# The quotients' steps of an attention kernel, one period each

## The chip, the cores and the metric

The kernel runs on one core of a Trainium2 chip. The metric is the device time of one execution in microseconds. Three runs of the kernel before took 1059.01, 1059.93 and 1061.18 us; the median is 1059.93. All times inside the execution are counted from its first instruction.

## The reference

Linear attention over 8 batches of 8 heads (576 positions, 64 dimensions, 128 features), and behind it a two-layer network on the 4608 rows that the attention gives. In the kernel the division of the attention stands in the middle of a long pipeline.

```python
def _attn_ref(q, k, v, w_phi):
    def phi(x):
        proj = np.einsum('bhsd,df->bhsf', x, w_phi)
        proj = proj - np.max(np.abs(proj), axis=-1, keepdims=True)
        return np.concatenate([np.exp(proj), np.exp(-proj)], axis=-1)
    q_p, k_p = (phi(q), phi(k))
    kv = np.einsum('bhsf,bhsd->bhfd', k_p, v)
    z = np.sum(k_p, axis=2)
    num = np.einsum('bhsf,bhfd->bhsd', q_p, kv)
    den = np.einsum('bhsf,bhf->bhs', q_p, z)[..., None] + 1e-06
    return (num / den)

def _moe_ref(x, w_in, w_out):
    h = x @ w_in
    return (h - np.tanh(h)) @ w_out
```

## The kernel before

Two heads of one batch make a unit; there are 32 units, numbered from 0. The attention stage is a software pipeline over the units. `ramp` starts the first three, `period(i)` for i from 3 to 31 does one step each of several units, `drain` ends the last five and starts the matrix stage. The order of the instructions on each engine is the order in which the program writes them (`manual_schedule`), so each engine and SyncE's DMA queue work strictly in that order.

In `period(i)` unit a = i is projected by TensorE (`project`, L327) and centred by VectorE (`centre`, L345 and L346); unit c = i - 1 gets its exponentials on ScalarE (`k_exp`, `q_exp`), its kv product on TensorE (`kv`, L409) and its key sums: GpSimd adds five blocks with four additions (`kadd`, L419 to L422), and one period later TensorE sums over the partitions (`ksum`, L428). Unit p = i - 2 gets its numerator (`num`, L456). Unit r = i - 3 gets its denominator (`denom`, L470).

From there the quotients run. `denom_copy` (ScalarE, L487) writes the denominators to the tile `dd`, of which there is one. `den_recip_load` (SyncE, L492) moves them to `dn`, spread over 128 partitions. `den_recip` (VectorE, L497) makes the reciprocals `rn`, `den_store` (SyncE, L502) writes them to DRAM as `rr`, `den_spread` (SyncE, L507, two DMAs) reads them back as `rb`, each head's row repeated over 64 partitions; there is one `rb`. `den_mul` (GpSimd, L510) multiplies the numerator `d` by `rb`, and `x_store` (SyncE, L513) writes the product to DRAM. The numerator comes to `d` by `num_copy` (ScalarE, L483); there are three buffers `d`, and a fourth for every fourth unit.

Before the change these steps lie in the periods of a unit u as follows. Load, reciprocal and store of the quotients are in period u + 3: the reciprocal is VectorE's last instruction of the period, and behind it stands the centring of the next one. The spread is in period u + 4, in SyncE's queue behind the load of dn. The product and its store are in period u + 5: the product stands on GpSimd ahead of the additions, the store at the head of SyncE's queue, ahead of the qk load.

SyncE's queue also holds the loads of q and k (`load`, L303, two periods ahead), of v (`load_v`, L307), of the raw weights (`dec_load`, L267 and L272) and, by `aside_at`, the stores of prepared weights (L112). The raw weights are decoded on ScalarE and VectorE (`dec_0` to `dec_3`); GpSimd prepares sums of weights between its other work (L168), and near the end sums of the stored products (`x0_sum`). `dn`, `rn` and the raw weights have two buffers each.

In the matrix stage (`frame`, one after another) the last two units' reciprocal, store, spread, product and store are put in by `hooks`.

Of the kernel before, what the change touches and what calls it, by code (L numbers as in the profile page):

```python
# [33 lines left out]
def tile_linear_attention_moe(  # L34
# [192 lines left out]
    with ExitStack() as c1:  # L227
# [287 lines left out]
        units = []  # L515
# [144 lines left out]
            k_exp(c, 0)  # L660

        def period(i):
            a, c, p, r, q, o = (unit(i - n) for n in range(6))
            w = dec[i - 3]
            dec.append(dec_load(i - 2))
            if i > 3:
                num_copy(r)
            k_exp(c, 1)
            if o:
                den_mul(o)  # L670
                x_store(o)
            if i + 2 < NU:
                load(units[i + 2])
            project(a, "jat")
            centre(a, "jt")
            kadd(c)
            ksum(p, p.pc[:, 0:F])
            ksum_copy(p)
            pu = bank()
            denom(r, pu)  # L680
            denom_copy(r)
            den_recip_load(r)
            if q:
                den_spread(q)
            if i > 3:
                load_v(a)
            aside_at(i, 2)
            aside_at(i, 3)
            kv_turn(p)
            ksum_turn(p, p.pc[:, F : 2 * F])  # L690
            kv_turn_copy(p, nc.scalar.copy)
            ksum_turn_copy(p)
            dec_0(w, a.pt)
            if i < NU - 1:
                aside_at(i, False)
            aside_at(i, True)
            q_turn(c)
            q_turn_rest(c, pu)
            q_exp(c)
            q_exp_rest(c)  # L700
            centre(a, "a")
            k_exp(a, 0)
            kv(c)
            kv_copy(c)
            dec_1(w)
            dec_2(w)
            dec_3(w)
            if r:
                den_recip(r)
                den_store(r)  # L710
            num(p)

        splits, lows, early_u = [], {}, {}

        def drain():
            o, q, r, p, c = units[-5:]

            def op(m):
                lows[m] = x_op(0, m, nc.vector)

            def pt_bank():
                return ps_t.tile([P, 2, 512], F32, tag="pt", name="pt")

            k0 = order[5]
            k_exp(c, 1)
            dec.append(dec_load(NU - 2))
            den_mul(o)
            ksum(p, p.pc[:, 0:F])
            ksum_copy(p)
            pu = bank()  # L730
            denom(r, pu)
            denom_copy(r)
            den_recip_load(r)
            ring_store(k0, 2)
            x0_sum(3)
            kadd(c)
            x_store(o)
            den_spread(q)
            kv_turn(p)
            ksum_turn(p, p.pc[:, F : 2 * F])  # L740
            kv_turn_copy(p)
            ksum_turn_copy(p)
            v = dec[NU - 3]
            dec_0(v, pt_bank())
            num_copy(r)
            x0 = xop[0][0]
            nc.scalar.copy(x0[:, 0], f32(x0[:, 1]))
            dec_1(v)
            dec_2(v)
            dec_3(v)  # L750
            x_low(nc.vector, x0, f32(x0[:, 1]))
            den_recip(r)
            den_store(r)
            q_turn(c)
            q_turn_rest(c, pu)
            q_exp(c, (0,))
            kv(c)
            kv_copy(c)
            q_exp(c, (1,))
            q_exp_rest(c)  # L760
            c0.close()
            xoa = ctx.enter_context(tc.tile_pool(name="xoa", bufs=1, side="right", reuse_waits="tile"))
            for s in XO_NEXT:
                xop_pool[s] = xoa
            ps_ab.append(ctx.enter_context(tc.tile_pool(name="ps_ab", bufs=1, side="right", reuse_waits="tile", space=PSUM)))
            num(p)
            kv_turn(c)
            kv_turn_copy(c)
            num_copy(p)
            pu = bank()  # L770
            denom(p, pu)
            denom_copy(p)
            den_recip_load(p)
            x1 = xop[0][1]
            nc.vector.tensor_copy(x1[:, 0], f32(x1[:, 1]))
            x_low(nc.vector, x1, f32(x1[:, 1]))
            w = dec[NU - 2]
            dec_0(w, pt_bank())
            dec_1(w)
            op(2)  # L780
            num(c)
            dec_2(w)
            dec_3(w)
            ksum(c, pu[:, 0:F])
            ksum_copy(c)
            den_mul(q)
            x_store(q)
            den_spread(r)
            op(3)
            lows[2]()  # L790
            bank_ab(0, ps_ab[0], "AB")
            product(A[0], 0, 0, 0, True)
            ksum_turn(c)
            u = early_u[0, "u1"] = wpool.tile([P, DM], F32, tag="w", name="u1_0")[:, 0:HT]
            nc.scalar.copy(u, A[0][:, 0:HT])
            ksum_turn_copy(c)
            product(Bk[0], 0, 1, 1, True)
            op(4)
            den_mul(r)
            x_store(r)  # L800
            num_copy(c)
            denom(c, bank())
            denom_copy(c)
            splits.extend(wo_split(f, nc.vector) for f in range(4))
# [10 lines left out]
    with ExitStack() as c2:  # L815
# [371 lines left out]
        def hooks(g, k):  # L1187
            q = NFP * g + k
            h = collections.defaultdict(list)
            nxt = g + 1  # L1190

            def op(at, g, m, low_at):
                keep = []
                h[at].append(lambda: keep.append(x_op(g, m, nc.vector)))
                h[low_at].append(lambda: keep[0]())

            if q + 2 < NQ:
                for n, at in enumerate(("a2", "a5", "end")):
                    h[at].append(lambda n=n: ring_load(q + 2, n))
            if g and k == 0:  # L1200
                op("a4", g, 6, "a6")
            if g and k == 1:
                for t, at in enumerate(("a2", "a2", "a3", "a5", "a5", "a6")):
                    h[at].append(lambda t=t: evict(g - 1, t, nc.vector if t == 1 else nc.scalar))
            if nxt < NG:
                if k == (2 if g else 4):
                    h["end" if g else "a2"].append(lambda: x_loads(nxt))
                if 4 <= k < 7:
                    for n, at in (((0, "a3"), (1, "end")), ((2, "a3"),), ((3, "a3"),))[k - 4]:
                        h[at if g else "end"].append(lambda n=n: x_sum(nxt, n))  # L1210
                    op("a4" if g else "end", nxt, k - 4, "a6" if g else "end")
                if k == 7:
                    op("a2", nxt, 3, "a3")
                    op("a4", nxt, 4, "a6")
                    op("end", nxt, 5, "end")
            if g == 0:
                for p in PREP.values():
                    for kk, at, names in (
(2, "end", "s1 s3 s2 s4"),
                        (3, "a3", "h2 l2 h4"),  # L1220
                        (3, "end", "l4 h6"),
                        (4, "a3", "l6"),
                        (4, "end", "h0 l0"),
                    ):
                        if k == kk:
                            h[at].extend(p[nm] for nm in names.split())
                for kk, at, n in ((3, "a6", 1), (4, "a6", 2), (5, "a1", 0)):
                    if k == kk:
                        h[at].append(lambda n=n: ring_store(NFP - 1, n))
                for kk, at, f in ((2, "end", LATE.d0), (3, "a7", LATE.d1), (5, "a7", LATE.d2), (6, "a7", LATE.d3)):  # L1230
                    if k == kk:
                        h[at].append(f)
                split = {}
                for n, at in enumerate(("a6", "a7")):
                    f = 2 * k + n

                    def hi(f=f):
                        split[f] = wo_split(f, nc.vector)
                        split[f][0]()

                    h["a0"].append(hi)
                    h[at].append(lambda f=f: split[f][1]())
            for n, kk in ((2, 2), (1, 4)):
                if g == 1 and k == kk:
                    h["start"].append(lambda n=n: (den_recip(units[-n]), den_store(units[-n]), den_spread(units[-n])))
                if g == 1 and k == kk + 1:
                    h["end"].append(lambda n=n: (den_mul(units[-n]), x_store(units[-n])))
            return h
# [102 lines left out]
```

## Time and profile before

| | |
|---|---|
| median of the three runs shown | 1059.93 us |
| profiled execution, its own time | 1059.23 us |
| its span, first to last instruction | 1057.4 us |
| around the span | 1.8 us |
| TensorE busy | 1042.4 us, 99% |
| VectorE, ScalarE, GpSimd busy | 870.2, 792.1, 272.8 us |
| attention stage, periods 4 to 31 | begins at 33.03 us; period 31 begins at 284.19 us |
| granted TensorE clock | 0.999 |

The busy time of TensorE is close to the whole span, but its matmuls are pipelined, and a wait shows less as idle time than as a later start of the next period. GpSimd works in the attention stage nearly alone: of the 40 slices of the span the last 27 show 0 tenths for it. In rows of the profile PE is TensorE, PEld its weight loads, DVE VectorE, ACT ScalarE, POOL GpSimd and SP SyncE; a q behind the name is the engine's sequencer or queue.

### The profile page before, as it was taken

How to read it: one execution, taken by the hardware profiler on the slowest of the kernel's cores; microseconds unless marked ns; L12 is line 12 of the kernel's file. 1: busy time of each engine (PE TensorE's matmuls, PEld its weight loads, DVE VectorE, ACT ScalarE, POOL GpSimd, SP SyncE). 2: the span in 40 equal slices, each digit the busy share in tenths (PEclk: the TensorE clock that was granted, in tenths of full speed). 3: DMA queues.
4: the chain of work that ended last, by engine and by line, in shares of the span. 5: the costliest groups of instructions: out<-in, count | busy, mean ns of one | idle time of the engine just before them, and what ended most of it. 6: DMA issues, size and time to landing. Idle time of an engine off the chain costs nothing.

```text
span 1057.4 us, 19349 instructions
## 1 busy us (share of the span) xinstructions
PE 1042.4 (99%) x7484; PEld 874.0 (83%) x7484; DVE 870.2 (82%) x1086; ACT 792.1 (75%) x1281; POOL 272.8 (26%) x233
## 2 busy tenths in 40 slices
PE   8999999999989999999999999999999999999998
PEld 6666666666668998999999999999999999999997
DVE  7899888889979899878887788867887778877776
ACT  5888888988878778766777666776677667776665
POOL 4799899989960000000000000000000000000000
PEclk9999999999999999999999999999999999999999
DMA  5789999999847653464335433345334543353311
GB/s 166 205 233 282 264 271 288 267 272 270 253 142 263 201 187 103 159 216 144 121 120 190 167 131 122 120 169 179 128 106 156 199 137 113 120 180 109 123 47 60
DMA packets 75738, 184.59 MB, mean 175 GB/s; under 512 B 15744, under 2 KB 30464, under 8 KB 75648
## 3 DMA queue, kind: packets, MB, share of 16 engines
q1 hardware_dynamic: 75360, 183.17, 53.9%
q8 instruction: 59, 0.97, 0.4%
q14 instruction: 31, 0.25, 0.1%
q10 hardware_dynamic: 288, 0.20, 0.1%
HBM read 149.49 MB, written 33.70 MB: 173 GB/s over the span
## 4 chain that ended last, share of the span: by engine, by line
PE 82%; DMA 7%; DVE 5%; ACT 2%; POOL 2%; issue 1%; SPq 1%; ACTq 0%; DVEq 0%; POOLq 0%
PE A L142 18%; PE B L142 14%; PE po L987 12%; PE po L988 12%; PE po L993 12%; DMA dn<-dd 4%; PE po L456 3%; PE pc L409 3%; DVE t L346 2%; PE pj L327 2%; PE pa L327 2%; PE pu L470 2%; DVE m L345 1%; DMA rb<-rr 1%; DMA rr<-rn 1%
## 5 line engine op out<-in xcount | busy, mean ns | idle before, releaser
L142 PE MATMUL A<-xo,wr 128*128 128x384 f32 x1152 | 231.5, 337 | 0.0
L142 PEld LDWEIGHTS A<-xo,wr 128*128 128x128 f32 x1152 | 204.9, 188 | 11.4 <-ACT d L483 0.5
L911 ACT COPY u<-A 128x384 f32<-128x384 f32 x143 | 68.5, 479 | 142.6 <-PE A L142 142.2
L142 PE MATMUL B<-xo,wr 128*128 128x384 f32 x864 | 173.7, 337 | 0.0
L142 PEld LDWEIGHTS B<-xo,wr 128*128 128x128 f32 x864 | 152.5, 188 | 4.2 <-DVE hx L918 0.4
L987 PE MATMUL po<-who,ghx 128*128 128x512 f32 x288 | 112.3, 390 | 0.7 <-ACT hy L925 0.7
L987 PE MATMUL po<-who,ghy 128*128 128x512 f32 x288 | 112.3, 390 | 0.3 <-ACT ghy L962 0.3
L988 PE MATMUL po<-wlo,ghx 128*128 128x512 f32 x288 | 112.0, 389 | 0.0
L988 PE MATMUL po<-wlo,ghy 128*128 128x512 f32 x288 | 112.0, 389 | 0.0
L510 POOL TENSOR_TENSOR d<-d,rb 128x576 f32<-128x576 f32 x32 | 46.3, 1448 | 165.4 <-DMA rb<-rr 160.8
L950 DVE SCALAR_TENSOR_TENSOR s2y<-s2y,thy 128x768 f32<-128x768 f32 x48 | 46.0, 959 | 51.5 <-ACT thy L941 51.5
L398 ACT ACTIVATE kp<-t 64x256 f32<-64x256 f32 (+1 forms) x126 | 85.1, 722 | 2.1 <-DVE t L346 1.0
L993 PE MATMUL po<-who,glx 128*128 128x512 f32 x288 | 80.9, 389 | 0.0
L935 ACT ACTIVATE yx<-hx 128x768 f32<-128x768 f32 (+1 forms) x49 | 41.0, 836 | 52.9 <-DVE hx L918 52.9
L993 PE MATMUL po<-who,gly 128*128 128x512 f32 x282 | 79.3, 389 | 0.3 <-DVE gly L965 0.3
L409 PE MATMUL pc<-kp,v 128*64 128x256 f32 x640 | 76.1, 384 | 0.5 <-DMA v<-in_v 0.4
L456 PE MATMUL po<-qe,kv 128*64 128x288 f32 x512 | 69.0, 412 | 0.4
L993 PEld LDWEIGHTS po<-who,glx 128*128 128x128 f32 x288 | 54.0, 188 | 11.2
L947 DVE SCALAR_TENSOR_TENSOR s2x<-s2x,yx 128x768 f32<-128x768 f32 (+1 forms) x49 | 46.1, 941 | 20.4 <-ACT s2x L936 19.1
L993 PEld LDWEIGHTS po<-who,gly 128*128 128x128 f32 x282 | 52.8, 188 | 11.7 <-DVE gly L965 0.8
L987 PEld LDWEIGHTS po<-who,ghx 128*128 128x128 f32 x288 | 54.1, 188 | 8.8 <-ACT hy L925 1.1
L987 PEld LDWEIGHTS po<-who,ghy 128*128 128x128 f32 x288 | 54.1, 188 | 8.5 <-ACT ghy L962 0.7
(186 smaller groups left out, 2228.8 us busy)
## 6 DMA issues: line engine op xcount, KB each, us to landing
wr<-wd SPq DMA_DIRECT2D x92, 512.0 KB
wr<-wd SPq DMA_DIRECT2D x46, 768.0 KB
qk<-in_qkT SPq DMA_DIRECT2D x31, 576.0 KB
v<-in_v SPq DMA_DIRECT2D x32, 320.0 KB
rb<-rr SPq DMA_DIRECT2D x64, 144.0 KB
xs<-d SPq DMA_DIRECT2D x32, 288.0 KB
out<-o SPq DMA_DIRECT2D x35, 256.0 KB
rawi<-in_moe_w_in SPq DMA_DIRECT2D x16, 512.0 KB
```

The costliest lines, as they stand in the source:

```text
L142: nc.tensor.matmul(bank[:, 0:HT], w[:, a, n, cs], x[:, b, c, :], start=start and i == 0, stop=i == 5, skip_group_check=not start,)
L327: nc.tensor.matmul(bank[:, e, k * F : (k + 1) * F], u.qk[hs, a * P : (a + 1) * P], wph[hs, :], start=True, stop=True)
L398: nc.scalar.activation(u.kp[h, :, j, s, :], u.t[r][h, :, x, :], AF.Exp, scale=1.0 - 2.0 * s)
L409: nc.tensor.matmul(u.pc[e * D : (e + 1) * D, 0 : 2 * F], u.v[:, j, e, :], u.kp[:, e, j, :, :], start=(j == first), stop=(j == last))
L456: nc.tensor.matmul(u.po[e * D : (e + 1) * D, c, 0:CH], u.kv[:, s, e * D : (e + 1) * D], u.qe[:, e, s, c * CH : (c + 1) * CH], start=(s == ...
L510: pin(nc.gpsimd.tensor_tensor(u.d, u.d, u.rb, ALU.mult))
L911: nc.scalar.copy(t, A[q][:, 0:HT])
L947: nc.vector.scalar_tensor_tensor(z.s[:, s], z.s[:, s], GC, z.y[:, s], ALU.add, ALU.mult)
L950: nc.vector.scalar_tensor_tensor(z.s[:, s], z.s[:, s], GK, z.th[:, s], ALU.mult, ALU.mult)
L987: nc.tensor.matmul(po, z.gh[:, ts], wh, start=first, stop=False)
L988: nc.tensor.matmul(po, z.gh[:, ts], wl, start=False, stop=False)
L993: nc.tensor.matmul(po, z.gl[:, ts], wh, start=False, stop=last)
```

## The change

In `period` the steps of the quotients move. The reciprocal and its store now serve unit q = i - 4 and stand ahead of the decoding of the weights; the spread serves unit o = i - 5 and stands near the head of SyncE's queue; the product of unit o stands behind the additions; the store of the product serves unit z = i - 6 and stands ahead of the spread. The load of dn stays with unit r but goes behind the load of v and the weight stores. `drain` and `hooks` are changed to fit: the drain makes the reciprocals of units 28 and 29, and the matrix stage gets the spread, the product and the store of unit 29.

```diff
         def period(i):
-            a, c, p, r, q, o = (unit(i - n) for n in range(6))
+            a, c, p, r, q, o, z = (unit(i - n) for n in range(7))
...
             k_exp(c, 1)
+            if z:
+                x_store(z)
             if o:
-                den_mul(o)
-                x_store(o)
+                den_spread(o)
...
             kadd(c)
+            if o:
+                den_mul(o)
...
             denom_copy(r)
-            den_recip_load(r)
-            if q:
-                den_spread(q)
...
             aside_at(i, 3)
+            den_recip_load(r)
...
             kv_copy(c)
+            if q:
+                den_recip(q)
+                den_store(q)
             dec_1(w)
             dec_2(w)
             dec_3(w)
-            if r:
-                den_recip(r)
-                den_store(r)
             num(p)
...
         def drain():
-            o, q, r, p, c = units[-5:]
+            z, o, q, r, p, c = units[-6:]
...
             dec.append(dec_load(NU - 2))
-            den_mul(o)
+            x_store(z)
+            den_spread(o)
...
             kadd(c)
-            x_store(o)
-            den_spread(q)
+            den_mul(o)
...
-            den_recip(r)
-            den_store(r)
+            den_recip(q)
...
             den_recip_load(p)
+            den_store(q)
+            x_store(o)
+            den_spread(q)
...
             x_store(q)
-            den_spread(r)
...
-            den_mul(r)
-            x_store(r)
+            den_recip(r)
+            den_store(r)
             num_copy(c)
...
-            for n, kk in ((2, 2), (1, 4)):
+            for n, kk in ((3, 0), (2, 2), (1, 4)):
                 if g == 1 and k == kk:
-                    h["start"].append(lambda n=n: (den_recip(units[-n]), den_store(units[-n]), den_spread(units[-n])))
+                    h["start"].append(lambda n=n: (n < 3 and (den_recip(units[-n]), den_store(units[-n])), den_spread(units[-n])))
```

## Rows read from the trace of the kernel before

**Rows 1.** The page: the chain that ended last, shares of the span by line.
```profile
PE A L142 18%; PE B L142 14%; PE po L987 12%; PE po L988 12%; PE po L993 12%; DMA dn<-dd 4%; PE po L456 3%; PE pc L409 3%; DVE t L346 2%; PE pj L327 2%; PE pa L327 2%; PE pu L470 2%; DVE m L345 1%; DMA rb<-rr 1%; DMA rr<-rn 1%
```

**Rows 2.** Waits from 30 to 292 us: us in total, times, longest.
```profile
POOL d L510 <- DMA rb<-rr: 11.7, 16, 1.8
...
DVE rn L497 <- DMA dn<-dd: 9.1, 11, 1.3
```

**Rows 3.** Timeline of TensorE, first projections of five periods: start us, us, instruction.
```profile
33.03 0.38 PE L327 MATMUL pj<-wph,qk 64*128 64x128 f32 x2
...
60.31 0.38 PE L327 MATMUL pj<-wph,qk 64*128 64x128 f32 x2
...
209.42 0.38 PE L327 MATMUL pj<-wph,qk 64*128 64x128 f32 x2
...
219.39 0.38 PE L327 MATMUL pj<-wph,qk 64*128 64x128 f32 x2
...
284.19 0.38 PE L327 MATMUL pj<-wph,qk 64*128 64x128 f32 x2
```

**Rows 4.** Timeline of VectorE and ScalarE; in brackets the idle time before.
```profile
211.44 0.22 DVE L497 RECIPROCAL rn<-dn 128x9 f32<-128x9 f32 x1 [1.34 <-DMA dn<-dd]
...
287.91 0.50 ACT L487 ACTIVATE dd<-pu,bias_t 128x288 f32<-128x288 f32 x1 [0.70 <-PE pu L470]
...
289.91 1.23 DVE L346 TENSOR_TENSOR t<-pa,m 128x1024 f32<-128x1024 f32 x1
```

**Rows 5.** Timeline of SyncE's queue in one period: the issues, not the transfers.
```profile
211.68 0.32 SPq L502 DMA_DIRECT2D rr<-rn  x1
...
214.81 0.39 SPq L303 DMA_DIRECT2D qk<-in_qkT  x1
...
215.97 1.87 SPq L507 DMA_DIRECT2D rb<-rr  x2
217.90 0.58 SPq L307 DMA_DIRECT2D v<-in_v  x1
```

**Rows 6.** Chain from 30 to 292 us, DMA pieces: start, us until its waiter.
```profile
107.95 2.83 DMA rr<-rn
...
126.63 5.09 DMA rr<-rn
...
204.86 6.49 DMA dn<-dd
...
215.29 5.69 DMA dn<-dd
...
272.59 4.95 DMA rb<-rr
```

**Rows 7.** Timeline of ScalarE and GpSimd: exponentials, first addition.
```profile
214.33 1.30 POOL L419 TENSOR_TENSOR ss<-kp 128x512 f32<-128x512 f32 x1
...
284.97 2.00 ACT L398 ACTIVATE kp<-t 128x1024 f32<-128x1024 f32 x2
```

**Rows 8.** Timeline of the drain, several engines.
```profile
294.88 0.43 PE L428 MATMUL pc<-ss,ones 128*32 128x128 f32 x8 [1.52 <-POOL ss L422]
...
296.55 1.41 POOL L510 TENSOR_TENSOR d<-d,rb 128x576 f32<-128x576 f32 x1
...
304.69 1.86 POOL L422 TENSOR_TENSOR ss<-ss,kp 128x512 f32<-128x512 f32 x1
...
306.61 0.43 PE L428 MATMUL pu<-ss,ones 128*32 128x128 f32 x8 [1.09 <-POOL ss L422]
...
307.97 0.33 SPq L513 DMA_DIRECT2D xs<-d  x1
...
309.59 0.65 ACT L483 COPY d<-po 128x576 f32<-128x576 f32 x1
...
310.49 1.32 PE L142 MATMUL A<-xo,wr 128*128 128x384 f32 x6
```

**Rows 9.** Busy time of a period: PE, PEld, DVE, ACT, POOL, clock, DMA share, GB/s.
```profile
115.66:125.83 10.17, 9.29 (x119) 6.13 (x118) 8.33 (x12) 8.32 (x16) 9.33 (x10) 1.00 0.95 255
```

## The prediction

> **What bounds the kernel now.** I read the chain of waits of the whole span first: it is matrix work nearly throughout, with one foreign entry in front, the load dn<-dd with 4% of the span, some 40 us [rows 1]. That is not yet 40 us to win, because the chain follows a load back to its issue, past matrix work that ran meanwhile. So second the list of waits of the attention stage, which tells what the engines really lost: VectorE's reciprocal waited 9.1 us in 11 periods for that load, and GpSimd's product 11.7 us in 16 periods for the spread quotients [rows 2]. Third, TensorE's first projection of each period, as a ruler. From 33.03 to 60.31 three periods took 27.28 us, 9.093 each; the one that begins at 209.42 took 9.97 [rows 3], and in that one the reciprocal stood idle for 1.34 us before it ran at 211.44 [rows 4]. VectorE works in order and centres the next projections behind the reciprocal, so TensorE gets its transposes late. About half a microsecond of each such wait is swallowed (1.34 became 0.88), because VectorE is that far ahead of TensorE in a period without a wait. Over all: 284.19 - 33.03 = 251.16 us for 27 periods, against 27 x 9.093 = 245.51. **5.65 us** is all that TensorE loses in the steady periods.
>
> Why the load is late: it stands in SyncE's queue behind the store of the product and the big qk load. The one for the reciprocal at 211.44 was issued at 204.86 and ended 6.49 us later, the longest such piece of the chain; the next, issued at 215.29, took 5.69 [rows 4, 6]. Behind the last period lies a second limit: in the drain TensorE waits 1.52 us at 294.88 and 1.09 us at 306.61 for GpSimd's additions, which run behind a product of 1.41 us [rows 8].
>
> **The change, part by part.** Nothing is added to the steady periods: one reciprocal, one store, two spreads, one product and one store of the product each, as before. They move. Times below are from a period's first projection.
>
> *Reciprocal.* It runs one period after its load, behind the last centring. That ends at 289.91 + 1.23 - 284.19 = +6.95 [rows 3, 4]. The load of the period before is issued by SyncE behind spread, qk, v and up to two weight stores: the new quotient store leaves at +7.19 (6.95 + 0.22, then 0.02 as between 211.66 and 211.68) and lands R later, so the next period's spread starts at R - 1.90; with 1.87 for the spread, 0.39 for qk, 0.58 for v and 0.58 for each weight store as a bound, the load leaves at R + 2.10 and lands D later [rows 5]. R is 2.83 to 5.09, D 5.69 to 6.49 [rows 6]: at worst +13.7, and the reciprocal wants it at 9.09 + 6.95 = +16.0. The wait goes, with 2.4 us to spare; its 0.22 us now lies ahead of the weight decoding, whose result is needed a period later. What is late next on VectorE is TensorE's projection itself. Gain 5.65 us.
>
> *Spread at the period's head.* Before it, SyncE holds the weight load and the store of an already finished product; behind it queue qk, v, the weight stores and dn. It waits until the quotient store has landed, +0.9 to +3.2. qk left at 214.81, +5.4, before, because SyncE stood before the product's store until GpSimd had multiplied; now at most at R - 1.90 + 1.87 = +5.1. Two periods lie between that load and its use. Cost nothing; the cover is those buffers.
>
> *Product behind the additions.* The additions can start when ScalarE's exponentials are done, 284.97 + 2.00 - 284.19 = +2.8, where they started at 214.33, +4.9 [rows 7]. Four of 1.3 us end near +8.2. The spread lands by about +0.9..3.2 plus 4.95 [rows 6] and its second issue, 1.4: +7.3 to +9.6. GpSimd may idle 1.4 us before the product, a wait that it had before (11.7 us in 16). The product's store is a period later; its buffer is wanted by the number copy at the next period's start, some 7 us after. Nothing either way.
>
> *DMA work.* A period of 10.17 us with the engines 0.95 busy holds 9.66 us of transfers [rows 9], more than 9.09. There the stage cannot come down to the ruler: 0.57 us comes back. Bounds: nothing (buffers even it out) to 1.5 us (its neighbours too).
>
> *Drain.* Of the two products that stood before the additions of the last two units one goes behind them, 1.41 us. In the last but one period the product now precedes the weight and input sums instead, so I count 1.0 us of earlier end for the last additions (bounds 0 and 1.41). A new wait stands against it: the product of the unit numbered 27 now follows those additions (end E = 304.69 + 1.86 = 306.55), its store leaves at E + 1.45 as at 307.97, and the last unit's copy d<-po at 309.59 (E + 3.04) reuses its buffer. TensorE's product at 310.49 waits for that copy's bank [rows 8]. No row shows the landing of such a store; between its issue of 0.3 and the 2.83 of the quickest small store [rows 6] it costs 0 to 1.24 us. I take the middle, 0.6. Drain: -0.4, bounds -1.4 to +1.2. The product and the store of unit 29 move into the matrix stage, where GpSimd is idle; its reciprocal stays in the drain, later, and costs at most its 0.22 us, which I put at nothing.
>
> The addition at 304.69 took 1.86 us, the one at 214.33 1.30 [rows 7, 8]. The Trainium skill ("GPSIMD Engine Reference", 1. Specifications) says that GpSimd shares its SBUF interfaces with VectorE and contends with instructions that have two SBUF inputs; the trace agrees as far as the length of this row goes. By that rule the additions, now beside other VectorE work, could all take 1.86, which would leave 0.6 us less.
>
> **Sum.** -5.65 + 0.57 - 0.4 = -5.5 us. The profiled execution took 1059.23 (span 1057.4 and 1.8 around it), so 1053.7; the median shown is 0.70 higher, which makes 1054.4. I forecast 1054.1.
>
> **Rivals.** *A, the wait moves (chance 0.12).* Part of the wait comes back as a late spread or as full DMA engines. For it: 9.66 us of transfers in the longest period [rows 9]. Against: that is the longest, and the loads have one to two periods of lead. If half of the 5.65 stays: about 1057.
>
> *B, slower: SyncE's queue as a loop (0.08).* Spread, qk, v, weight stores and dn all stand behind one landing. dd has one buffer, so ScalarE's copy at 287.91, +3.72 [rows 4], may not start before dn has been read: R + 2.10 + D must stay under 9.09 + 3.72 = 12.81, R + D under 10.7. Behind that copy are the kv and key-sum copies that TensorE waits for. With both longest rows, 5.09 + 6.49 = 11.58, each of 25 periods is 0.87 longer, 22 us: 1076. The change loses from R + D = 10.71 + 5.5/25 = 10.93 on. Against: 2.83 + 5.69 = 8.5 are the lower rows. The Trainium skill ("DMA: Bandwidth & Descriptors", Latency and other measured facts) puts the fixed cost of a DMA at about 2 us, higher under load; with 2 us each the rival could not occur, but the rows show two to three times that.
>
> *C, no change (0.10).* The reciprocal's waits go, but the same half microsecond is lost elsewhere, because VectorE or the DMA engines were late anyway; 1059 to 1060. Against: the periods without a wait keep 9.09 with the same work. Here belongs also that the load, issued later, still comes too late; the 2.4 us speak against it.
>
> Forecast 0.70. Its own range is 1052.5 to 1056.5, from the bounds of the drain and of the DMA term. About 0.2% or 2.1 us is what a measurement of this kernel can tell from no change. Faster by more: the forecast and most of A, 0.81. Within: C and the rest of A, 0.11. Slower: B, 0.08. The range 1051.9 to 1057.6 takes in A.
>
> **What would show it.** Right: no idle time before the reciprocal, a ruler of 9.09 from the fifth period on, 245.5 to 246.5 us for the 27 periods; additions starting near +2.9; the product's idle time small; in the drain a short wait of the last copy d<-po for a store. Wrong: idle time of ScalarE before dd for a load (B), of TensorE for v or qk (A), or a ruler that stays at 9.3 with nothing waiting for dn (C).

## The result and the profile after: slower by 1.3%

The changed kernel takes 1074.65 us (median of 4 runs, 1071.52 to 1076.05) beside 1060.56 us of the kernel before on the same chip (4 runs): ratio 1.0128, 95% interval 1.0100 to 1.0156. Forecast were 1054.1 us and "faster". The case that came is rival B, which had a chance of 0.08, with a second loss in the drain that no rival named. One of the six runs of experiment 6 took 1292.98 us at a mean granted clock of 0.753, a slow run, and is left out of its median.

The profiled execution of the changed kernel has a span of 1074.3 us, 16.9 more than before. (It is the longest of the four, 1076.05 us, and the one before, 1059.23 us, lies under its median; between the medians it is 14.1.) Where the 16.9 us lie is read from TensorE's timeline, the first projections of the fifth period, of three neighbouring ones in the middle, and of the last. Columns: start us, us, instruction.

```profile
33.74 0.38 PE L327 MATMUL pj<-wph,qk 64*128 64x128 f32 x2
...
137.17 0.38 PE L327 MATMUL pj<-wph,qk 64*128 64x128 f32 x2
...
146.87 0.38 PE L327 MATMUL pj<-wph,qk 64*128 64x128 f32 x2
...
160.31 0.38 PE L327 MATMUL pj<-wph,qk 64*128 64x128 f32 x2
...
293.79 0.38 PE L327 MATMUL pj<-wph,qk 64*128 64x128 f32 x2
```

The 27 periods take 293.79 - 33.74 = 260.05 us against 251.16 [rows 3], 8.9 more, where 5.65 less were to be won. From the last period's start to the end of the span it is 1074.3 - 293.8 = 780.5 against 773.2, 7.3 more. The remaining 0.7 us lie ahead of the fifth period, where nothing of the change has run yet; in the kernels below that point lies between 33.2 and 34.1, so nothing is read into it. The period that starts at 137.17 takes 9.70 us, the one that starts at 146.87 takes 13.44, the longest.

The waits of the attention stage, 30 to 300 us (waiter, releaser: us in total, times, longest), to be held against [rows 2]:

```profile
ACT dd L487 <- DMA dn<-dd: 21.5, 13, 3.5
...
POOL d L510 <- DMA rb<-rr: 10.6, 11, 1.7
...
PE pu L367 <- ACT dd L487: 7.6, 9, 2.3
```

VectorE's reciprocal is gone from the list: 9.1 us in 11 waits before, none now. But the same load, dn, is waited for on another engine: ScalarE may not write the one dd buffer again before dn has been read from it, and TensorE waits for the bank behind that copy.

How the load comes to be so late stands in SyncE's queue just ahead of the longest period and in it (start, us, instruction; issues, not transfers):

```profile
142.71 1.10 SPq L507 DMA_DIRECT2D rb<-rr  x2
143.90 0.54 SPq L303 DMA_DIRECT2D qk<-in_qkT  x1
144.49 0.42 SPq L307 DMA_DIRECT2D v<-in_v  x1
144.96 1.05 SPq L112 DMA_DIRECT2D wd<-wr  x2
146.11 0.92 SPq L492 DMA_DIRECT2D dn<-dd  x1
147.13 1.32 SPq L502 DMA_DIRECT2D rr<-rn  x1
...
153.54 1.10 SPq L507 DMA_DIRECT2D rb<-rr  x2
```

and on VectorE and ScalarE at the same time (in brackets the idle time before, and what ended it):

```profile
144.40 0.21 DVE L497 RECIPROCAL rn<-dn 128x9 f32<-128x9 f32 x1
...
153.39 0.50 ACT L487 ACTIVATE dd<-pu,bias_t 128x288 f32<-128x288 f32 x1 [3.49 <-DMA dn<-dd]
```

The quotients are ready at 144.61. Their store does not leave then, because SyncE is still working off what stood behind the spread; it leaves from 147.13 to 148.45. The next spread needs that store landed and starts at 153.54, 5.1 us later. From spread to spread it is 10.83 us: 5.74 of issues, which follow each other without a gap, and 5.09 of landing. The period without a wait is 9.09 [rows 3]. That SyncE stands and waits for this landing is read from its own waits, 30 to 300 us, the changed kernel first and the kernel before second:

```profile
SPq L507 <- DMA rr<-rn: 65.5, 25, 4.3
...
SPq L507 <- DMA rr<-rn: 1.7, 3, 1.0
```

So the queue falls behind, period by period, until dn comes too late for ScalarE; that wait lengthens a period, the queue catches up, and it begins again.

In the drain, ScalarE, TensorE, GpSimd and SyncE show this:

```profile
316.56 0.43 PE L428 MATMUL pu<-ss,ones 128*32 128x128 f32 x8 [1.13 <-POOL ss L422]
...
318.42 1.14 SPq L507 DMA_DIRECT2D rb<-rr  x2
...
320.09 0.64 ACT L483 COPY d<-po 128x576 f32<-128x576 f32 x1 [0.44 <-DMA xs<-d]
...
323.49 1.40 POOL L510 TENSOR_TENSOR d<-d,rb 128x576 f32<-128x576 f32 x1 [5.59 <-DMA rb<-rr]
...
324.92 0.33 SPq L513 DMA_DIRECT2D xs<-d  x1
...
327.12 0.61 ACT L938 ACTIVATE s2x<-yx,bias_t 128x384 f32<-128x384 f32 x1 [5.58 <-DMA xs<-d]
...
328.56 3.89 PE L142 MATMUL A<-xo,wr 128*128 128x384 f32 x11 [4.39 <-ACT u L913]
```

Unit 28's spread leaves at 318.42, when the single rb buffer is free of unit 27; its product follows at 323.49, its store at 324.92. The matrix stage's first square, s2x, lies in memory that was this unit's d0 buffer, waits 5.58 us for that store, and ScalarE's copies of the banks queue behind it: TensorE stands 4.39 us. Before, the store of the same unit left at 307.97 [rows 8], and the square, at 311.67, did not wait for it.

### The profile page after: what moved, and what is told of

Same layout as the page of the kernel before. It is cut to its first block, busy times and chain, and to the rows that moved or that the text cites. A ratio compares the mean times of both kernels' runs of the same rounds, so it can differ in the third digit from the quotient of the medians.

```text
span 1074.3 us, 19314 instructions
## 1 busy us (share of the span) xinstructions
PE 1048.2 (98%) x7484; PEld 879.2 (82%) x7484; DVE 868.6 (81%) x1086; ACT 789.8 (74%) x1281; POOL 272.5 (25%) x233
## 4 chain that ended last, share of the span: by engine, by line
PE 81%; DMA 7%; DVE 5%; POOL 3%; ACT 2%; issue 1%; SPq 1%; ACTq 0%; DVEq 0%; POOLq 0%
PE A L142 18%; PE B L142 13%; PE po L989 12%; PE po L990 12%; PE po L995 12%; PE pc L409 4%; DMA rr<-rn 3%; PE po L456 3%; PE pj L327 2%; DMA dn<-dd 2%; DVE m L345 2%; DVE t L346 1%; PE pa L327 1%; DMA rawi<-in_moe_w_in 1%; PE pu L470 1%
## 5 line engine op out<-in xcount | busy, mean ns | idle before, releaser
L409 PEld LDWEIGHTS pc<-kp,v 128*64 128x64 f32 x640 | 43.4, 137 | 23.7 <-ACT ks L441 3.7
L345 DVE TENSOR_REDUCE m<-pj 128x8 f32<-128x1024 f32 x32 | 39.2, 1226 | 27.4 <-PE pj L327 27.4
```

The source lines that it names most:

```text
L345: nc.vector.tensor_reduce(m, x, AX.X, ALU.max, apply_absolute_value=True)
L409: nc.tensor.matmul(u.pc[e * D : (e + 1) * D, 0 : 2 * F], u.v[:, j, e, :], u.kp[:, e, j, :, :], start=(j == first), stop=(j == last))
```

## The experiments

Two theories on the periods went in. Q: the loss in the periods is made by the order of SyncE's queue, in which the quotient store stands behind the late spread and dn. S, the rival: a spread that waits for a landing at the head of the period is too late as such. (What the expectation of experiment 2 calls theory S is another one, on the drain.) The spans from the fifth to the last period's start ("27 periods": 251.16 before, 260.05 after) and from there to the end ("tail": 773.2 and 780.5) are read for every kernel as above, each from one execution; kernels whose periods are the same program differ in them by some 2 us (after 260.05, experiment 2 262.0; experiment 5 257.35, experiment 6 255.7). Times are compared with the kernel before as it ran beside each, hence the ratios. Edits are against the kernel after unless said otherwise; the code is cut, and lines of it are shortened.

**1. Reciprocal and its store early.**
```
 denom_copy(r)
+if q: den_recip(q)          # ahead of the last centring
 if i > 3: load_v(a)
+if q: den_store(q)          # ahead of weight stores and dn
 ...
-if q: den_recip(q); den_store(q)   # behind kv_copy(c)
```


> The changed kernel, but the reciprocal of unit i - 4 runs ahead of the last centring (near +4.2 of its period, not +6.9), and SyncE issues the quotient store behind the load of v, ahead of the weight stores and of the load of dn. Theory Q (SyncE's queue is a loop: quotient store, its landing, spread, qk, v, weight stores, dn, next quotient store; longer than 9.09 us): the store leaves near +5 and lands by +10, the next spread leaves by +2.5, dn by +7; ScalarE's waits before dd for dn fall from 21.5 us to under 3, the 27 periods take 245.5 to 248 us instead of 260.05, and the time falls by 11 to 14 us, to 1060 to 1064. Theory D (the transfers themselves are slower in the changed kernel, median landing of dn 5.1 us against 4.3, whatever stands in front): the waits before dd stay above 10 us, 1070 or more. Both: the loss of some 7 us in the drain stays.

1064.61 us (10 runs), ratio to before 1.0049 (1.0034 to 1.0063). 27 periods 282.97 - 33.59 = 249.38; the waits of ScalarE for dn fall from 21.5 us in 13 to:
```profile
ACT dd L487 <- DMA dn<-dd: 3.0, 2, 1.7
```
So 10.7 us come back in the periods; a period without a wait is 9.16 instead of 9.09 (27 x 0.07 = 1.9 us), probably because the reciprocal now precedes a centring. With that, periods and time end a little over what Q said (248 and 1064). The tail is 778.6, 5.4 over the kernel before. Q's mechanism holds, theory D's does not; the drain is a loss of its own.

**2. Drain: unit 28 with a second rb.** Its reciprocal and store move to the middle of the drain, its spread into a weight tile's memory, so that it need not wait for unit 27.
```
 kv_turn_copy(p)
+den_recip(q); den_store(q)
 ...
 dec_3(v)
+den_spread(q, second=True)
 ...
-den_recip(q) ... -den_store(q) ... -den_spread(q)
```


> The changed kernel with the drain alone altered: unit 28 gets its reciprocal and quotient store earlier and its spread in a second buffer (in the memory of the raw weights), so that its product follows that of unit 27 at once. Theory S (ScalarE's first square of the matrix stage waits 5.6 us for the store of unit 28, whose buffer lies where the square writes; TensorE then runs for a stretch at a granted clock of 0.62 to 0.69): the wait falls below 1.5 us, no slow stretch, from the last period's start to the end some 774 us instead of 780.5, time 1067 to 1069. Rival: the square waits for something else that this store only happens to follow, or the slow clock has its own cause; 1073 to 1075. The 27 periods stay near 260 us in both.

1070.56 us (4 runs), 1.0094 (1.0057 to 1.0130). The tail falls from 780.5 to 1070.3 - 295.2 = 775.1; s2x waits 2.1 us (under 1.5 was expected) and TensorE 0.9, and the granted clock stays at 1.00. The periods are as bad as after (262.0), which is why the time lies over the expected 1067 to 1069. So some 5.4 of the 7.3 us of the drain are that wait.

**3. The product alone** (against the kernel before: product behind the additions, its store a period later; spread, reciprocal and quotient store as before).
```
-if o: den_mul(o); x_store(o)
+if z: x_store(z)
 ...
 kadd(c)
+if o: den_mul(o)
```


> The kernel before with one part of the change alone: the product stands behind the additions and its store at the head of the next period; load, reciprocal, quotient store and spread stay where they were. Theory Q: SyncE no longer stands at the period's head until GpSimd has multiplied, so qk and dn leave about a microsecond earlier; the reciprocal's waits (9.1 us for dn) fall to under 4, the 27 periods take 246 to 249 us instead of 251.2, time 1055 to 1058. Rival P: the load of dn cannot leave earlier because ScalarE writes dd only at +4.3, or what is ahead of it in the DMA queues does not change; periods near 251, time 1059 to 1061. Rival R: the product behind the additions itself costs, GpSimd falls behind and TensorE waits for its additions; slower than 1062.

1084.0 us (4 runs), 1.0239 (1.0193 to 1.0286). 27 periods 270.2. The time lies where rival R had it (over 1062), but not by R's way: no wait of TensorE for the additions is in the list. The spread, which stands ahead of v in SyncE's queue, waits until the product has released the one rb buffer (57.8 us in 25 of SyncE's own waits), and v and the quotient store wait with it; waits of the engines from 30 to 304 us:
```profile
DVE rn L497 <- DMA dn<-dd: 26.8, 21, 2.6
...
PE pc L409 <- DMA v<-in_v: 14.1, 12, 1.9
ACT d L483 <- DMA xs<-d: 13.7, 8, 2.3
```
So a late product holds up the queue of the engine that issues for it, and by its late store the copies into d.

**4. The spread behind qk, v and the weight stores,** just ahead of dn; the product follows it.
```
 if z: x_store(z)
-if o: den_spread(o)
 ...
-if o: den_mul(o)             # behind kadd(c)
 ...
 aside_at(i, 3)
+if o: den_spread(o); den_mul(o)
 den_recip_load(r)
```


> The changed kernel, but SyncE issues the spread behind qk, v and the weight stores, just ahead of dn, so that it stands waiting for the quotient store's landing with these loads already out. Theory Q: the loop is shorter by the 1.5 to 2.1 us that these issues take; dn leaves near +6.5, the waits before dd fall from 21.5 us to under 5, the 27 periods take 246 to 250 us, time 1060 to 1065. GpSimd's product waits longer for the spread, up to +11, at no cost to TensorE. Theory D: periods near 260, time 1072 to 1076.

1101.03 us (4 runs), 1.0392 (1.0360 to 1.0423), over both theories; 27 periods 282.0. The waits for dn shrink, though not under 5 us, but the product waits for the spread, the additions queue behind it, and the product's store at SyncE's head waits for the product (108.6 us in 25 of SyncE's own waits): by these waits another loop, longer than the first. Waits of the engines from 30 to 316 us:
```profile
POOL d L510 <- DMA rb<-rr: 49.8, 25, 3.1
...
PE pc L428 <- POOL ss L422: 18.3, 14, 2.6
...
ACT dd L487 <- DMA dn<-dd: 8.8, 6, 1.9
```

**5. dn ahead of v and the weight stores.**
```
 denom_copy(r)
+den_recip_load(r)
 if i > 3: load_v(a)
 aside_at(i, 2); aside_at(i, 3)
-den_recip_load(r)
```


> The kernel after, with one line moved: the load dn of the denominators stands right behind the qk load in SyncE's queue, ahead of the v load and the weight stores; reciprocal, quotient store, spread and product stay where the change put them. Theory Q (the loss in the periods comes from the order dn, then quotient store, in SyncE's queue: a late dn makes the store late, the store's landing makes the spread late, the spread makes the next dn late): with about 4.5 us for a landing of the store and 5.1 for dn, dn leaves at about +5.5 and lands at +1.5 of the next period, 2 us ahead of ScalarE's copy dd; the store leaves at +7.2. The 27 periods take 246 to 249 us, ScalarE's waits for dn fall from 21.5 us under 4, and the time is 1059 to 1063, the drain's loss of some 7 us staying. Rival S (any spread at the head of the period delays the whole queue enough): the waits for dn stay over 12 us and the time is over 1066.

1067.61 us (6 runs), 1.0090 (1.0067 to 1.0113); 27 periods 257.35. Q's numbers missed, and the time is the one that rival S had (over 1066), but not by S's way: the waits for dn fall to 4.5 us in 4, where S had over 12. The loop stays as long wherever dn stands in it, and the wait went over to v, 6.2 us in 7. From SyncE and TensorE around the longest period:
```profile
174.57 0.54 SPq L303 DMA_DIRECT2D qk<-in_qkT  x1
175.20 0.58 SPq L492 DMA_DIRECT2D dn<-dd  x1
175.83 0.46 SPq L307 DMA_DIRECT2D v<-in_v  x1
176.35 0.42 SPq L112 DMA_DIRECT2D wd<-wr  x1
176.87 0.38 SPq L502 DMA_DIRECT2D rr<-rn  x1
...
184.02 1.10 SPq L507 DMA_DIRECT2D rb<-rr  x2
...
182.67 4.07 PE L409 MATMUL pc<-kp,v 128*64 128x256 f32 x20 [2.20 <-DMA v<-in_v]
```
The quotients of that store were ready at 172.06; it left at 176.87, behind everything that the late spread had held.

**6. The same with unit 28 early in the drain,** its spread into the keys' memory, its product ahead of unit 27's, both behind the last additions.
```
+den_recip(q); den_store(q)          # drain's head
 den_recip_load(r)
+den_spread(q, second=True)
 ...
 kadd(c)
+den_mul(q); x_store(q)
 den_mul(o)
+x_store(o)
 ...
-den_recip(q) ... -den_store(q); x_store(o); den_spread(q) ... -den_mul(q); x_store(q)
```


> The kernel before this one (dn ahead of v and of the weight stores), and in the drain unit 28 is finished one step earlier: its reciprocal and store at the drain's head, its spread into memory of the keys that is free by then (so that it need not wait for the one rb buffer), its product ahead of that of unit 27, both behind the last additions. Theory: the 5.6 us that ScalarE waited in the drain for the store of unit 28, and the low clock behind that idle time, go, 5.5 to 7 us: 1053 to 1057, faster than both kernels. Rival: the drain's loss is the clock or the later additions, not that wait: 1058 to 1062.

1065.68 us (5 of 6 runs), 1.0082 (1.0060 to 1.0104), over what was expected; 27 periods 255.7, tail 778.9. The wait only changed its place: TensorE stands 3.54 us at 319.8, now because ScalarE's copy of the last unit waits for the store of unit 27, which went second.

**7. That drain with the first experiment's early reciprocal.** Edits of both.

> The kernel after with the reciprocal ahead of the last centring (as in the first experiment) and the drain's unit 28 finished one step earlier. Theory: the first experiment's 1064.6 less 5.5 to 7 for the drain: 1057.5 to 1059.5, level with the kernel before, because the reciprocal on VectorE ahead of the centring costs about 1.8 us over 27 periods. Rival: the two corrections do not add, because the drain's wait only moves to the next store: over 1061.

1061.22 us (8 runs), 1.0041 (1.0026 to 1.0055), over the theory's range: the rival came. 27 periods 248.56, tail 777.0, for the same reason as in 6 (TensorE stands 2.84 us there).

**8. The reciprocal's step alone.** Spread behind dn, product and its store at the period's head, as before, all one period later; drain as in 6.
```
-if z: x_store(z)
-if o: den_spread(o)
+if z: den_mul(z); x_store(z)
 ...
-if o: den_mul(o)             # behind kadd(c)
 ...
 denom_copy(r)
+den_recip_load(r)
+if o: den_spread(o)
 if i > 3: load_v(a)
-den_recip_load(r)            # behind the weight stores
```


> Only the first step of the change, the reciprocal and its store a period later; the spread stands behind dn as in the kernel before, the product and its store at the head of the period as there, all one period later; dn ahead of v; the drain as in the two other kernels with unit 28 finished early. Theory: with the spread behind dn its wait for the quotient store is over before SyncE comes to it, so that no loop closes, and what was forecast comes: 27 periods in 245.5 to 248, 1054 to 1058 in all. Rival: the store of the product at SyncE's head, which waits for GpSimd, delays qk, dn and v as it did in the kernel before, and with another unit behind it the queue is as late as in the change: over 1061.

1058.84 us (12 runs), 1.0004 (0.9993 to 1.0014): level, and 0.8 over the theory's range. But the 27 periods take 246.17 us, within it:
```profile
34.12 0.38 PE L327 MATMUL pj<-wph,qk 64*128 64x128 f32 x2
...
280.29 0.38 PE L327 MATMUL pj<-wph,qk 64*128 64x128 f32 x2
```
No wait for dn is left. What is won is lost again behind the last period (tail 775.6), where TensorE stands 3.47 us for the copy that waits for unit 27's store.

**9. The same with unit 27's product ahead of unit 28's,** and its spread at the drain's head.
```
 x_store(z)
+den_spread(o)
 ...
-den_mul(q); x_store(q); den_mul(o); x_store(o)
+den_mul(o); x_store(o); den_mul(q); x_store(q)
```


> The kernel of the reciprocal alone (1058.8) with the drain's two products in the other order: unit 27 first, its spread at the drain's head, then unit 28. There ScalarE's copy of the last unit waited 3.6 us for the store of unit 27, whose buffer it reuses, and TensorE 3.5 us behind it. Theory: that wait falls to about 0.4, and the matrix stage's square, which reuses the memory of unit 28, waits about 2 instead, of which TensorE loses 0.9 as in the third experiment: 1056 to 1058. Rival: what is lost behind the last period is not these waits: 1058.5 to 1060.

1055.51 us (5 runs) beside 1060.65 of before: 0.9946 (0.9932 to 0.9961), faster than both kernels, and a little under the expected 1056. 27 periods 246.42, tail 773.3, level with before. The waits of the copy and of the square are down to 0.43 and 0.56 us, and of TensorE's 4.39 us are left 0.54:
```profile
305.37 0.64 ACT L483 COPY d<-po 128x576 f32<-128x576 f32 x1 [0.43 <-DMA xs<-d]
...
308.56 0.62 ACT L941 ACTIVATE s2x<-yx,bias_t 128x384 f32<-128x384 f32 x1 [0.56 <-DMA xs<-d]
...
310.01 2.36 PE L142 MATMUL A<-xo,wr 128*128 128x384 f32 x12 [0.54 <-ACT u L916]
```

**10. As 9, unit 28's product in the memory of an input tile.**
```
+if u.i == NU - 4: u.d = pq.tile([P, PC], F32, tag="qk")[:, 0:S]
```


> As the kernel with unit 27 first, and unit 28's product lies in the memory of an input tile that is free by then, so that the matrix stage's square does not reuse it. Theory: neither wait is left, 1055 to 1057, about 3 us under the kernel before. Rival: the memory of the input tile is reused as early by the matrix stage's operands, and the wait only changes its place: 1057 to 1060.

1060.84 us (12 runs), 1.0003 (0.9990 to 1.0015). The rival came, 0.8 over its range: a cast of the matrix stage's operands, which reuses that memory, waits 6.89 us for the store, and the tail is 781.4.

**11. The quotient store issued by ScalarE** in the periods. The expectation puts it behind ScalarE's last exponentials; the edit puts it ahead of the first of the next unit, so that it leaves from +7.1 on and not at +8.3.
```
 centre(a, "a")
+if q: den_recip(q); den_store(q, nc.scalar)
 k_exp(a, 0)
 ...
-if q: den_recip(q); den_store(q)   # behind kv_copy(c)
```


> The kernel after with one thing changed: in the steady periods the quotient store is issued by ScalarE, behind its last exponentials (about +8.3), and not by SyncE. All else, the spread at the period's head and dn behind v and the weight stores too, stays. Theory Q2 (the loop is spread, what SyncE issues behind it, quotient store, landing, spread; the place of dn alone did not open it): the store no longer waits in SyncE's queue, leaves at about +8.3 in each period, lands near +13, and the spread follows at about +4 of the next period and does not slide: 27 periods in 246 to 250 us, ScalarE's waits for dn under 5 us in all, 1061 to 1065 with the drain's loss of some 7 us. Rival S2 (a spread that has to wait for a landing at the head of the period is too late as such): the 27 periods stay above 255 and the time above 1068.

1071.22 us (4 runs), 1.0091 (1.0074 to 1.0109); 27 periods 256.64. These are the numbers of rival S2, not of Q2. The spread no longer slides on from period to period (it leaves at +1.3 to +5.3), but the waits for dn stay, 17.4 us in 11. Taking the store out of the loop was not enough, with dn behind v and the weight stores.

**12. Edits 5 and 11 together.**

> The kernel after with both single edits of two experiments before: the quotient store of the steady periods is issued by ScalarE (there it left at +7.1 to +8.5, and the spread behind its landing at +3.3 to +6), and dn stands ahead of v and the weight stores. Theory Q3 (two things together make the loss: the loop through SyncE's queue, and a dn that stands behind v and the weight stores, some 1.7 us, after a spread that waits for a landing of 5 to 7 us): neither is left, dn leaves near +6 and lands near +10.5, v near +6.7 and lands near +11.5: 27 periods in 246 to 250 us, and 1060 to 1064 with the drain's loss. Rival S2 (a spread that waits at the head of the period is too late as such): v comes too late instead, 27 periods above 254, over 1066.

1062.24 us (12 runs), 1.0026 (1.0015 to 1.0037); 27 periods 281.03 - 33.73 = 247.30. SyncE and ScalarE in one period:
```profile
104.65 0.33 ACTq L502 DMA_DIRECT2D rr<-rn  x1
...
110.74 1.10 SPq L507 DMA_DIRECT2D rb<-rr  x2
111.94 0.54 SPq L303 DMA_DIRECT2D qk<-in_qkT  x1
112.57 0.59 SPq L492 DMA_DIRECT2D dn<-dd  x1
113.20 0.46 SPq L307 DMA_DIRECT2D v<-in_v  x1
...
113.75 0.34 ACTq L502 DMA_DIRECT2D rr<-rn  x1
```
The next store leaves 9.10 us after the last one, whatever SyncE does, and the spread follows 6.09 us after the store's start. Periods and time are as the theory had them, and no wait for dn is left. S falls: the spread leaves at +1.3 to +5.2, mostly near +3.5, and the periods still come within 1.8 us of the ruler, if the store does not stand behind the spread and dn stands soon behind it.

So the cause in the periods is shown, in two parts: the queue as a loop, and dn behind v and the weight stores. One edit alone (5, 11) leaves 256 to 257 of the 260 us; both give 247.3. The place of dn is a cause only behind a late spread: experiment 1 left it where it was and still won nearly as much, because its store left at +4.6 to +6.3 and the next spread at +1.2 to +4.0. That the losses in the periods and in the drain are the whole is read from the sums (8.9 and 7.3 of 16.9); experiment 9 shows besides that the reciprocal's own step keeps its gain where both are avoided: periods shorter by 4.7, tail level.

## Why the prediction was wrong, step by step

*What bounds the kernel: right.* The 5.65 us of the reciprocal's waits were there to be had. Experiments 8 and 9 win 4.99 and 4.74 of them; the forecast, with its DMA term of 0.57, was 5.08. That this comes so near is in part luck. The DMA term was put on one period, the one from 115.66 to 125.83, which could not come down to the ruler for its 9.66 us of transfers; in experiments 8 and 9 that period takes 9.09, and what is missing lies in four and five others of 9.25 to 9.32, which were not taken apart.

*Reciprocal: right in itself.* It runs at +6.86 (forecast +6.95), at +7.23 in the period that starts at 137.17, with nothing to wait for.

*The quotient store "leaves at +7.19": this step failed.* It took the reciprocal's end for the store's start, though on SyncE the store stands behind the spread and all that the spread holds up. In periods where nothing is late it does leave at +7.10, but of the period shown it left at 147.13 - 137.17 = +9.96, 0.26 us into the next one. The step was a chain through one period where it should have been a round. The prediction's own terms are spread 1.87, qk 0.39, v 0.58 and a weight store 0.58; with some 0.6 for the issue of dn, the quotient store's 0.32 and its landing R of 2.83 to 5.09, which belong to the round, they make 7.2 to 9.4 us, already past 9.09 at the upper end and with one weight store only. The sum R + 2.10 + D was then started from a point that itself moves. Rival B had the place, and the sign that it named, idle time of ScalarE before dd, is what came; but its condition, R + D over 10.7, was written without the queue and therefore got 0.08. That its price of 1076 lies near the 1074.65 is luck: its 22 us were all to come from the periods, which lost 14.5 against the ruler (260.05 - 245.51), and the drain made up part of the rest.

*R and D: R was too low, the second thing that failed.* R is the time from the quotient store's start to its landing, D the same for dn. The chain of waits after, 30 to 300 us, has among others (start, us until its waiter; before: [rows 6]):
```profile
146.11 7.18 DMA dn<-dd
...
248.82 3.73 DMA rr<-rn
...
264.93 5.32 DMA dn<-dd
...
283.18 6.71 DMA rr<-rn
```
D is 5.32 to 7.18, about as taken; R is 3.73 to 6.71 where 2.83 to 5.09 was taken from a kernel in which the store left at another point of the period. From a store's start to the spread that waits for it the median is 5.5 us in the changed kernel, and still 5.4 in experiment 12, where SyncE's queue does not delay the store. With the store from +7.1 on and 6.3 for the same median, dn behind v and the weight stores comes too late now and then: experiment 11. The Trainium skill ("DMA: Bandwidth & Descriptors", Latency and other measured facts), cited for a fixed cost of about 2 us, higher under load, does not help here: no landing in these rows comes near 2 us.

*Product behind the additions: half right.* Where the product of the period before is not late, the additions start at +2.86 (forecast +2.8); else later, up to +5.6. They did not lengthen beside other VectorE work: the first one takes 1305 ns in the mean of 27 (1307 before), the long rows of 1.86 stay in the drain, so that the 0.6 us that the prediction set beside its sum did not come. "Nothing either way" holds only while no wait for that product stands in a queue with loads (experiments 3 and 4).

*Drain: one term right, one not reached, one missing.* The 1.0 us of earlier additions comes where the periods run smoothly: TensorE waits 0.38 us for those of the last but one unit in experiment 7 and 0.48 in 9, 1.52 before [rows 8], and the sum over the last additions starts 21.4 us after the last period's start, 22.4 before. In the changed kernel it does not come (1.82 and 22.8); there the additions of the last period start late, at +5.56. That it is the product's new place which brings it is not shown, since experiment 9 has it with the product ahead of the additions. The new wait of the copy d<-po is 0.44 us (forecast 0.6), of which TensorE loses 0.28. Missing is the second reuse: unit 28's product in d0, whose memory passes to the matrix stage. The prediction follows the products of units 27 and 29 and says nothing of unit 28; and "move into the matrix stage, where GpSimd is idle", said of unit 29, looks at the engine, not at the store and who waits for its landing.

*What the forecast was worth.* Its 5.5 us are there to be had, but with the first step of the change alone, and with a drain of its own: experiment 9 is 5.1 us under the kernel before between the medians, 0.54% or some 5.7 by the ratio. The other steps, costed at nothing in the periods, took back more than three times as much.

What stays open: why R is 0.9 to 1.6 us longer at the ends of its range, which is only seen and not taken apart, and a kernel with edits 5, 11 and 9's drain was not run.

## What to carry to other kernels

Where an in-order queue issues both a load that waits for a store and, later, that same store, add up everything between them once around, landing included, and compare it with the period: a round longer than the period slides until something breaks, even if every single step has slack. When the last products of a stage are put off, follow their stores to the memory they leave, not only the engine that computes them. And try the parts of a change apart: here one was worth 0.5%, and the others together cost more than three times that.

## What was unexpected of the hardware

The 4.39 us in which TensorE stood idle in the drain cost more than themselves, because the granted clock fell in them to the lower of its two levels, 1.2 GHz (0.50; 1.00 is 2.4 GHz), and was still there when the work came back. Stretches of the changed kernel (us, length, busy time of PE, PEld, DVE, ACT, POOL, granted clock, DMA share, GB/s):
```profile
324.00:326.00 2.00, 0.17 (x1) 0.00 (x0) 0.00 (x0) 0.00 (x0) 0.90 (x1) 1.00 0.12 47
326.00:328.00 2.00, 0.00 (x0) 0.00 (x0) 0.23 (x1) 0.88 (x2) 0.00 (x0) 0.56 0.65 232
...
332.00:333.00 1.00, 1.00 (x5) 1.00 (x4) 0.00 (x0) 0.29 (x2) 0.00 (x0) 0.50 1.08 365
333.00:334.00 1.00, 1.00 (x7) 1.00 (x6) 0.00 (x0) 1.00 (x3) 0.00 (x0) 0.97 1.03 371
```
TensorE is idle from 324.17 to 328.56, and the clock is at 0.50 from 328 until 333. By an estimate from the two levels, the 4.4 us of work from 328.56 on would have taken half of that at full clock, so some 2.2 us more are lost: 4.39 + 2.2 = 6.6, most of the 7.3 us of the tail. The same matmuls show it one by one: 11 of them took 3.89 us there, 0.35 each, and 12 took 2.36, 0.20 each, in experiment 9, where the stretch from 310 to 315 has a clock of 1.00. So a wait in the list of waits can be worth half as much again as it says. It need not be: in experiment 8 TensorE stands 3.47 us in the drain and the clock reads 1.00 on both sides, while in experiment 7 it stands 2.84 us and the clock is at 0.50 from 312 to 314. What decides between the two was not taken apart.
